# The first batch's first transform folded on VectorE and TensorE, with another order behind it

## The chip, the cores and the metric

The kernel runs on one core of one Trainium2 chip. The metric is the device time of one execution in microseconds (us); lower is better. A core has five engines that run their own instruction queues: TensorE (PE in the rows, with PEld its weight loads), VectorE (DVE), ScalarE (ACT), GpSimd (POOL) and SP (SyncE), which here only issues DMAs. Every engine takes its instructions in program order, and a semaphore wait of one instruction holds back those behind it.

## The reference

Eight batches of 3072 positions with 256 channels pass through three layers; all is fp32.

```python
X = np.fft.rfft(x, axis=1)                       # x: (8, 3072, 256)
y = np.fft.irfft(X * (filt_r + 1j * filt_i)[None], n=3072, axis=1)
...
h = np.maximum(x @ w_in, 0.0)                    # (24576, 256) @ (256, 2048)
x = h * h @ w_out                                # (24576, 2048) @ (2048, 256)
...
logits = x @ phi                                 # 32 slots, 8 experts of 4
d = softmax(logits, axis=0)                      # over all tokens
slot_input = (d.T @ x).reshape(8, 4, 256)
slot_out[e] = np.maximum(slot_input[e] @ w1[e], 0) @ w2[e]
out = softmax(logits, axis=1) @ slot_out
```

The second and third layers see the whole (24576, 256) array.

## The kernel before, in words

The kernel has a start-up of about 60 us, a main loop over 384 pairs of w_in column blocks (`pair`, with `layer`, `square`, `turn_h`, `logit`), and an end with the experts. The transforms of batches 1 to 7 are spread over the main loop as streams of events; batch 0 has to be transformed in the start-up, because the main loop's first chunk needs it. Only batch 0, with the constants it uses, is touched here.

The 3072-point transform is done as 128 x 24: index n1 has 128 values (on partitions), n2 has 24. Batch 0 passes these stages, each an event with a time key:

- `load_u` loads x by n2 into tiles `x` (line 160); `mm_at` multiplies each 128 x 128 block of x, as the stationary operand, with the 128 x 128 matrix `ca` (line 275): this is the first transform, and its result comes out with the channels on partitions. `evac_at` copies it into `AT` (lines 284 and 286).
- `mm_t` turns blocks of `AT` back (line 294), `evac_t` copies (line 299); group i of eight holds 16 of the 128 first frequencies.
- `mm_b` is the 24-point transform (line 309), `filt` four VectorE products with the filter for each group i (line 320), `join` the sums on GpSimd (line 329), `mm_g` the inverse 24-point transform (line 349), `evac_g` four ScalarE copies (line 362). Group 7 has no join: its `mm_g` has twice the matmuls.
- `store_g` stores the groups' rows to DRAM tensors `Gu` (groups 0 to 5) and `Gz` (6 and 7) (line 371), and `load_gi` loads the tile `gi` back in another order (line 378). Then `mm_ai` (line 501), `lead_ai` (ScalarE, line 510) and `rest_ai` (VectorE, line 522) make the main loop's first operand `xo`, and `layer` begins (lines 615 to 622); `square` is the relu (line 627). A `warm` of matmuls without use (lines 402 and 494) runs at the beginning and while gi is awaited.

Beside these, the start-up converts the weights, which arrive as 64-bit floats. For each tile of w_in and w_out `conv` runs one ScalarE copy (line 987, k = 0) and then five VectorE operations (lines 944, 945, 948, 949, 1002, k = 1 to 5); `split_wi` then makes a high part on ScalarE (line 1014) and a low part on VectorE (line 1012). `WI` and `WO` hold their time keys; the first two tiles of w_in are converted in halves.

The order on each engine is written by hand. `put0(t, fn, ...)` files an event under the key t, and at the end all events are called in the order of their keys; a key is not a time that anything waits for, it only says what stands ahead of what in program order. Of the keys of `fft_events`, F(i) = 20 + 2.45 i.

PSUM has eight banks; `bank0(k)` names one, and a matmul group waits until the last reader of its bank is done. `mm_at(u)` takes bank u % 8, `mm_t` banks 4 to 7, `mm_b(i)` two of banks 0 to 3, `mm_g(i)` four banks by a table.

The batches behind the first are folded already (`fold_x`, `mm_a`): a row n1 and the row n1 + 64 are added for the even frequencies and subtracted for the odd ones, which leaves two products over 64 rows.

Of the kernel before, what the change touches and what calls it, by code (L numbers as in the profile page):

```python
# [6 lines left out]
F32 = mybir.dt.float32  # L7
# [31 lines left out]
def body(tc, x, cA, cAf, fwp, fwd, ivp, inv, flt, cst, w_in, w_out, phi, w1, w2, out):  # L39
# [23 lines left out]
    def F(i):  # L63
# [4 lines left out]
        ([.35, 27.6], [[16.6, 17.1, 17.11, 17.12, 17.13, 17.14], [34.2, 40.4, 40.41, 40.42, 40.43, 40.44]], 47.2, 47.58),  # L68
        ([30.1], [[41, 46, 46.1, 46.2, 46.3, 46.4]], 47.3, W + .1),
        ([W + 2.2], [[W + 4] + [W + t for t in (5.9, 6.4, 7.3, 7.8, 8.5)]], W + 9.1, W + 10.1),  # L70
# [62 lines left out]
    def fft_events(b, pl, put, TA, TB, TG, n, st):  # L133
# [22 lines left out]

        def load_u(u, m=2):
            sl, n = divmod(2 * u, 4)
            st["x", sl] = st["big"][sl // 4][:, sl % 4]
            sync.dma_start(out=st["x", sl][:, n:n + m], in_=xv[:, 2 * u:2 * u + m, :])  # L160

# [108 lines left out]
        def mm_at(u):  # L270
            st["at", u] = p = bank0(u % 8)
            for k in range(2):
                for m in range(2):
                    o = 128 * (2 * k + m)
                    pe.matmul(
                        p[:, o:o + 128], st["x", u // 2][:, 2 * (u % 2) + m, 128 * k:128 * k + 128], st["ca"],
                        start=True, stop=True,
                    )

        def evac_at(u):  # L280
            o = st["AT"][:, :, :, 2 * u:2 * u + 2]
            p = st.pop(("at", u)).rearrange("p (k n q) -> p k q n", k=2, n=2)
            if u == 2:
                vec.tensor_copy(o, p)
            else:
                act.activation(out=o, in_=p, func=ACTF.Copy)

# [46 lines left out]
        def mm_g(i):  # L334
            v = st.pop(("iv", i))
            st["g", i] = p = [bank0(k) for k in ((4, 5, 6, 7), (0, 1, 4, 5), (2, 3, 6, 7))[(i > 3) + (i > 5)]]
            if i < 7:
# [66 lines left out]
        if b == 0:  # L404

            st["wz"] = cv.tile([128, 512], F32, tag="wx", name="wz", bufs=1)
            st["ca"] = pl().tile([128, 128], F32, name="ca")
            put(0.01, load_ca)
            put(0.05, warm, st["wz"][:, 0:128], 7)
            st["AT"] = one("AT", [128, 2, N1, 32])  # L410
            st["big"] = [G["big"].tile([128, 4, 4, D], F32, tag=f"h{n}", name="x", bufs=1) for n in "AB"]
            put(0.04, lambda: vec.memset(st["AT"][:, :, :, N2:], 0.0))
            for u in range(6):
                put(.2 + .01 * u, load_u, u)
            for u in range(6, 12, 2):
                put((.27, .28, .31)[u // 2 - 3], load_u, u, 4)
            put(.32, load_k, C_ID, C_SS)
            put(.46, load_k, C_I, C_ID)
            put(.461, load_k, C_SS, C_END)
            for u in range(12):  # L420
                put(4.2 + .98 * u, mm_at, u)
                put(5.4 + .98 * u, evac_at, u)
            put(.37, load_c, 0)
            put(.45, load_c, 1)
            put(.43, load_i, 0)
            put(.455, load_i, 1)
            put(29.3, negate)
            for i in range(8):
                put((.38, .4, .42, .44)[i] if i < 4 else F(i - 4) + 2.6, load_f, i)
                T = (16.8, 17.2, 20, 22.4, 24.9, 25.3, 27.4, 27.8)[i]  # L430
                for s in range(2):
                    put(T + .1 * s, mm_t, i, s)
                    put(T + .3 + .1 * s, evac_t, i, s)
                put(F(i) - 1.2, mm_b, i)
                for r in range(2):
                    put(F(i) + 1.25 * r, filt, i, r)
                    if i < 7:
                        put(F(i) + 1.3 + 1.25 * r, join, i, r)
                put((29.85, 32.3, 34.75, 37.2, 39.9, 41.5, 44.6, 40.5)[i], mm_g, i)
                T = (31.1, 33.6, 36.1, 38.6, 41.2, 44.7, 45.9, 42.4)[i]  # L440
                for c in range(4):
                    put(T, evac_g, i, c)
                put(T + 1.25, store_g, i)
            put(45.0, load_gi, sync, 0, "Gu", 0, 64)
            return
# [31 lines left out]
    def out_events(b, st, late):  # L477

        def load_g(g):
            if b + g:  # L480
                t = G["mlp"].tile([128, 4, D], F32, tag="gin", name="gin", bufs=2)
                src, o = (st["G1"], 0) if (b, g) == (0, 1) else (st["G"], 4 * g - 8 * (b == 0))
                sync.dma_start(out=t, in_=src[:, o:o + 4, :])
                st["gi", g] = t
                return
            st["load_gi"](sync, 0, "Gu", 64, 96)
            st["load_gi"](sync, 96, "Gz", 16, 32)
            st["load_gi"](sync, 96, "Gz", 0, 16)

# [977 lines left out]
def _constants():  # L1467
# [11 lines left out]
    cA = np.tile(a[:64].reshape(64, 2, 64), (2, 1, 1))  # L1479
    cAf = a.reshape(N1, 8, 2, 4, 2).transpose(0, 1, 3, 2, 4).reshape(N1, N1)  # L1480
    ci = np.where(ri[None, :] == 0, np.cos(ph), -np.sin(ph)).T.copy()
# [134 lines left out]
```

## Time and profile before

| | |
|---|---|
| median of 3 runs | 1836.63 us (1831.43 to 1837.27) |
| profiled execution | 1833.53 us |
| its span, first to last instruction | 1831.6 us |
| mean granted TensorE clock | 0.997 of full speed |
| TensorE busy | 1799.2 us, 98% of the span |
| VectorE, ScalarE, GpSimd busy | 66%, 57%, 43% |

All times in rows are microseconds from the span's start. A timeline row merges neighbouring instructions of one line; its second number is from the first one's start to the last one's end. fp32 matmuls appear as two instructions each, apart from transposes. The granted clock is in parts of 2.4 GHz.

### The profile page before, as it was taken

Reading aid. Unit: us, or ns where it says so; the run is one execution under the profiler, and the core shown is the slowest. Engines: PE = TensorE matmul, PEld = TensorE weight load, DVE = VectorE, ACT = ScalarE, POOL = GpSimd, SP = SyncE. Lnnn points to the kernel's source line nnn. Section 1 sums busy time; section 2 is a strip of 40 time slices with the busy share of each in tenths; the row PEclk is TensorE's granted clock in tenths of the full one; section 3 lists DMA queues with packets and bytes.
Section 4 is the critical chain, followed back from the end, with each engine's and each line's share of the span. In section 5 each row is a group of like instructions: output and inputs, shape, how many; then the busy total and the mean of one; then the engine's idle time right before and its main releaser. Section 6 shows DMA issues by size and latency. Waiting matters only on the chain.

```text
span 1831.6 us, 41877 instructions
## 1 busy us (share of the span) xinstructions
PE 1799.2 (98%) x16338; PEld 1195.2 (65%) x16338; DVE 1200.7 (66%) x2252; ACT 1046.5 (57%) x1942; POOL 782.1 (43%) x818
## 2 busy tenths in 40 slices
PE   9899999999999999999999999999999999999986
PEld 7666666666676666666666666666666676666555
DVE  7856766776576656667567666666566756556567
ACT  6755555555654664655555566465555565555556
POOL 4144543544354534445345543445344433333234
PEclk9999999999999999999999999999999999999999
DMA  8669989888888888888878888788888766675889
GB/s 315 207 182 285 254 231 266 255 220 226 250 211 227 222 250 214 220 233 232 235 210 231 222 234 243 207 224 237 236 214 226 189 177 179 171 201 155 302 305 384
DMA packets 236419, 425.00 MB, mean 232 GB/s; under 512 B 25536, under 2 KB 94784, under 8 KB 233408
## 3 DMA queue, kind: packets, MB, share of 16 engines
q1 hardware_dynamic: 235352, 421.13, 80.8%
q8 instruction: 130, 2.13, 0.5%
q10 hardware_dynamic: 728, 1.15, 0.2%
q14 instruction: 65, 0.53, 0.1%
q0 software_dynamic: 144, 0.07, 0.0%
HBM read 151.71 MB, written 77.59 MB: 125 GB/s over the span
## 4 chain that ended last, share of the span: by engine, by line
PE 93%; DVE 2%; DMA 2%; ACT 1%; issue 1%; SPq 1%; POOL 0%; ACTq 0%; DVEq 0%
PE p L620 20%; PE p L622 19%; PE p L621 19%; PE L L689 10%; PE S L820 5%; PE sd L820 3%; PE sd L309 3%; PE sd L228 3%; PE sd L175 2%; PE sd L537 1%; PE y L537 1%; DVE ct L1245 1%; PE pt L1234 1%; PE pt L1447 1%; PE sd L349 1%
## 5 line engine op out<-in xcount | busy, mean ns | idle before, releaser
L648 DVE STREAM_TRANSPOSE hT<-h 128x512 f32<-128x512 f32 x736 | 490.4, 694 | 320.3 <-ACT h L629 302.0
L631 POOL TENSOR_TENSOR h<-h 128x512 f32<-128x512 f32 x375 | 391.5, 1044 | 591.9 <-ACT h L627 559.1
L627 ACT ACTIVATE h<-p 128x512 f32<-128x512 f32 x768 | 458.8, 597 | 323.2 <-PE p L622 305.1
L620 PE MATMUL p<-xo,wiH 128*128 128x512 f32 x1534 | 619.6, 404 | 0.8 <-ACT h L627 0.6
L622 PE MATMUL p<-xo,wiL 128*128 128x512 f32 x1534 | 605.9, 395 | 0.0
L621 PE MATMUL p<-xo,wiH 128*128 128x512 f32 x1534 | 605.2, 395 | 0.1
L620 PEld LDWEIGHTS p<-xo,wiH 128*128 128x128 f32 x1534 | 288.3, 188 | 126.3 <-issue 35.8
L622 PEld LDWEIGHTS p<-xo,wiL 128*128 128x128 f32 x1534 | 288.5, 188 | 68.3
L621 PEld LDWEIGHTS p<-xo,wiH 128*128 128x128 f32 x1534 | 288.8, 188 | 61.9 <-DVE xo L522 0.5
L629 ACT ACTIVATE h<-h 128x512 f32<-128x512 f32 x393 | 248.4, 632 | 12.5
L329 POOL TENSOR_TENSOR u<-u 128x256 f32<-128x256 f32 x224 | 160.9, 740 | 131.0 <-DVE u L320 117.2
L689 PE MATMUL L<-h,wf 128*32 128x512 f32 x1536 | 187.9, 599 | 0.5 <-ACT h L629 0.4
L320 DVE TENSOR_TENSOR u<-sd,f 128x512 f32<-128x512 f32 x240 | 151.8, 670 | 39.1 <-PE sd L309 39.0
L571 POOL TENSOR_TENSOR xo<-gin,xo 128x512 fp32r<-128x512 f32 x90 | 116.9, 1310 | 101.6 <-ACT xo L564 101.6
L556 DVE TENSOR_TENSOR gin<-gin,sd 128x512 f32<-128x512 f32 x90 | 61.8, 687 | 92.6 <-ACT gin L547 91.1
L547 ACT ACTIVATE gin<-y 128x512 f32<-128x512 f32 x28 | 16.7, 597 | 161.0 <-PE sd L537 161.0
L689 PEld LDWEIGHTS L<-h,wf 128*32 128x32 f32 x1536 | 40.1, 109 | 94.9 <-issue 92.1
L820 PE MATMUL S<-hd,eT 128*32 128x512 f32 x896 | 101.3, 592 | 0.0
L166 POOL TENSOR_TENSOR f<-f 128x512 f32<-128x512 f32 x42 | 54.2, 1291 | 85.6 <-DVE u L165 79.0
L564 ACT ACTIVATE xo<-gin 128x512 fp32r<-128x512 f32 x90 | 53.3, 621 | 41.3 <-DVE gin L556 41.3
L796 DVE STREAM_TRANSPOSE eT<-et 32x128 f32<-32x128 f32 x184 | 72.3, 393 | 1.9
L820 PEld LDWEIGHTS S<-hd,eT 128*32 128x32 f32 x896 | 29.1, 110 | 67.0 <-issue 67.0
(168 smaller groups left out, 1732.2 us busy)
## 6 DMA issues: line engine op xcount, KB each, us to landing
hd<-hT SPq DMA_DIRECT2D x736, 256.0 KB
f<-flt SPq DMA_DIRECT2D x28, 1024.0 KB
gin<-G SPq DMA_DIRECT2D x47, 512.0 KB
out<-w1t SPq DMA_DIRECT2D x22, 1024.0 KB
f<-x SPq DMA_DIRECT2D x84, 256.0 KB
S<-f SPq DMA_DIRECT2D x42, 512.0 KB
f<-S SPq DMA_DIRECT2D x112, 192.0 KB
G<-f SPq DMA_DIRECT2D x112, 192.0 KB
```

The costliest lines, as they stand in the source:

```text
L320: vec.tensor_tensor(out=u, in0=p.rearrange("p (h d) -> p h d", d=D), in1=f[:, 2 * r + k:2 * r + k + 1, :].to_broadcast([128, 2, D]), op=AL ...
L329: gps.tensor_tensor(out=a[:, h, :], in0=a[:, h, :], in1=b[:, 1 - h, :], op=ALU.add if h else ALU.subtract)
L571: gps.tensor_tensor(out=lo, in0=st["gi", g][:, k::2, :], in1=hi, op=ALU.subtract)
L620: pe.matmul(p, wh, x[:, 0, kk, :], start=(kk == 0), stop=False)
L621: pe.matmul(p, wh, x[:, 1, kk, :], start=False, stop=False)
L622: pe.matmul(p, wl, x[:, 0, kk, :], start=False, stop=(kk == 1))
L627: act.activation(out=h, in_=p, func=ACTF.Relu, scale=2.0 ** -8)
L629: act.activation(out=h, in_=h, func=ACTF.Square)
L631: gps.tensor_tensor(out=h, in0=h, in1=h, op=ALU.mult)
L648: vec.transpose(hT[c, f // 8][:, f // 4 % 2, :, o:o + 128], h2[P, k].rearrange("p (b t) -> p b t", b=4))
L689: pe.matmul(lg[c][32 * n:32 * n + 32, :], wf[:, f, :], h2.pop((P + n // 2, n % 2)), start=(f < 4), stop=(f >= FT - 4), tile_position=(0, 3 ...
L820: pe.matmul(S[32 * n:32 * n + 32, :], e[:, 32 * t:32 * t + 32], v, start=(t == 0), stop=(t == 3), tile_position=(0, 32 * n),)
```

## The change

For batch 0 the first transform is folded as well. x is loaded in six units u, each with rows n1 under 64 and over 64 side by side, and with four n2, two on the upper and two on the lower 64 partitions (12 loads of 256 KB instead of six of 256 KB and three of 512 KB). For u = 0 to 3 VectorE adds and subtracts the two halves (`fold_u`), and TensorE multiplies the results by 64 x 64 tiles. For u = 4 and 5 TensorE does the sum itself: it accumulates both halves, with a third block of `ca` that holds the negated odd columns. Each unit fills two PSUM banks, and ScalarE evacuates both (`evac_at(u, g)`; before, unit 2 of twelve was copied by VectorE).

The keys of `mm_t`, `evac_t`, `mm_b`, `mm_g` and `evac_g` are earlier; the groups' last three come as 5, 7, 6 instead of 7, 5, 6, and groups 5 to 7 use other banks. The ScalarE copy of the third tile of w_in has key 43 instead of 41. gi is loaded in two pieces: 96 rows of `Gu` ahead of group 6's store in the queue, and 32 rows of `Gz`; before, it was 64 and 32 rows of `Gu` and twice 16 of `Gz`.

```diff
--- before.py
+++ after.py
@@ -66,7 +66,7 @@
     WI = [
         ([.26, .3], [[8.4, 9.9, 9.91, 9.92, 9.93, 9.94], [13.26, 13.3, 13.31, 13.32, 13.33, 13.34]], 20.4, 40.3),
         ([.35, 27.6], [[16.6, 17.1, 17.11, 17.12, 17.13, 17.14], [34.2, 40.4, 40.41, 40.42, 40.43, 40.44]], 47.2, 47.58),
-        ([30.1], [[41, 46, 46.1, 46.2, 46.3, 46.4]], 47.3, W + .1),
+        ([30.1], [[43, 46, 46.1, 46.2, 46.3, 46.4]], 47.3, W + .1),
         ([W + 2.2], [[W + 4] + [W + t for t in (5.9, 6.4, 7.3, 7.8, 8.5)]], W + 9.1, W + 10.1),
     ]
     WO = [
@@ -154,10 +154,19 @@
                         out=t[64 * g:64 * g + 64, k].rearrange("p (h n) d -> p h n d", h=2), in_=xh[:, :, n:n + 2, :]
                     )
 
-        def load_u(u, m=2):
-            sl, n = divmod(2 * u, 4)
-            st["x", sl] = st["big"][sl // 4][:, sl % 4]
-            sync.dma_start(out=st["x", sl][:, n:n + m], in_=xv[:, 2 * u:2 * u + m, :])
+        def load_u(u):
+            st["x", u] = t = st["big"][u // 4][:, u % 4]
+            for g in range(2):
+                n = 4 * u + 2 * g
+                sync.dma_start(
+                    out=t[64 * g:64 * g + 64].rearrange("p (h n) d -> p h n d", h=2), in_=xh[:, :, n:n + 2, :]
+                )
+
+        def fold_u(u):
+            t = st["x", u]
+            st["eo", u] = [small(k) for k in ((("u0", "u1"), ("u2", "u3"), ("u4", "u5"), ("u6", "u7"))[u])]
+            for o, op in zip(st["eo", u], (ALU.add, ALU.subtract)):
+                vec.tensor_tensor(out=o, in0=t[:, 0:2], in1=t[:, 2:4], op=op)
 
         def fold_x(s, k):
             t = st["x", s][:, k]
@@ -268,22 +277,32 @@
                 sync.dma_start(out=f[:, r:r + 2], in_=flt[i, :, r:r + 2])
 
         def mm_at(u):
-            st["at", u] = p = bank0(u % 8)
+            st["at", u] = p = [bank0((2 * u + g) % 8) for g in range(2)]
+            ca, t = st["ca"], st["x", u]
+            if ("eo", u) in st:
+                terms = [[(a, 0, 64 * e)] for e, a in enumerate(st.pop(("eo", u)))]
+            else:
+                terms = [[(t, 0, 64 * e), (t, 2, 128 * e)] for e in range(2)]
             for k in range(2):
-                for m in range(2):
-                    o = 128 * (2 * k + m)
-                    pe.matmul(
-                        p[:, o:o + 128], st["x", u // 2][:, 2 * (u % 2) + m, 128 * k:128 * k + 128], st["ca"],
-                        start=True, stop=True,
-                    )
-
-        def evac_at(u):
-            o = st["AT"][:, :, :, 2 * u:2 * u + 2]
-            p = st.pop(("at", u)).rearrange("p (k n q) -> p k q n", k=2, n=2)
-            if u == 2:
-                vec.tensor_copy(o, p)
-            else:
-                act.activation(out=o, in_=p, func=ACTF.Copy)
+                for n in range(2):
+                    for e, term in enumerate(terms):
+                        for m, (a, h, c) in enumerate(term):
+                            for g in range(2):
+                                rows = slice(64 * g, 64 * g + 64)
+                                for d in range(2):
+                                    o, q = 128 * (2 * k + n) + 64 * e, 128 * k + 64 * d
+                                    pe.matmul(
+                                        p[g][64 * d:64 * d + 64, o:o + 64], a[rows, h + n, q:q + 64],
+                                        ca[rows, c:c + 64],
+                                        start=(m == 0), stop=(m == len(term) - 1), skip_group_check=True,
+                                        tile_position=(64 * g, 64 * d),
+                                    )
+
+        def evac_at(u, g):
+            n = 4 * u + 2 * g
+            o = st["AT"][:, :, :, n:n + 2]
+            p = st["at", u][g].rearrange("p (k n q) -> p k q n", k=2, n=2)
+            act.activation(out=o, in_=p, func=ACTF.Copy)
 
         def mm_t(i, s):
             st["tp", i, s] = p = bank0(4 + (2 * i + s) % 4)
@@ -333,7 +352,7 @@
 
         def mm_g(i):
             v = st.pop(("iv", i))
-            st["g", i] = p = [bank0(k) for k in ((4, 5, 6, 7), (0, 1, 4, 5), (2, 3, 6, 7))[(i > 3) + (i > 5)]]
+            st["g", i] = p = [bank0(k) for k in ((4, 5, 6, 7), (0, 1, 4, 5), (6, 7, 0, 1), (6, 7, 0, 1), (2, 3, 4, 5))[max(0, i - 3)]]
             if i < 7:
                 y = [st.pop(("y", i, r)) for r in range(2)]
                 terms = [[(v[:, r, k, :], y[r][:, k, :]) for r in range(2)] for k in range(2)]
@@ -404,22 +423,24 @@
         if b == 0:
 
             st["wz"] = cv.tile([128, 512], F32, tag="wx", name="wz", bufs=1)
-            st["ca"] = pl().tile([128, 128], F32, name="ca")
+            st["ca"] = pl().tile([128, 192], F32, name="ca")
             put(0.01, load_ca)
             put(0.05, warm, st["wz"][:, 0:128], 7)
             st["AT"] = one("AT", [128, 2, N1, 32])
             st["big"] = [G["big"].tile([128, 4, 4, D], F32, tag=f"h{n}", name="x", bufs=1) for n in "AB"]
             put(0.04, lambda: vec.memset(st["AT"][:, :, :, N2:], 0.0))
             for u in range(6):
-                put(.2 + .01 * u, load_u, u)
-            for u in range(6, 12, 2):
-                put((.27, .28, .31)[u // 2 - 3], load_u, u, 4)
+                put((.2, .21, .22, .27, .28, .31)[u], load_u, u)
             put(.32, load_k, C_ID, C_SS)
             put(.46, load_k, C_I, C_ID)
             put(.461, load_k, C_SS, C_END)
-            for u in range(12):
-                put(4.2 + .98 * u, mm_at, u)
-                put(5.4 + .98 * u, evac_at, u)
+            for u in range(6):
+                T = 4.2 + 1.6 * u
+                if u < 4:
+                    put(T - .2, fold_u, u)
+                put(T, mm_at, u)
+                for g in range(2):
+                    put(T + 1.2 + .1 * g, evac_at, u, g)
             put(.37, load_c, 0)
             put(.45, load_c, 1)
             put(.43, load_i, 0)
@@ -427,21 +448,21 @@
             put(29.3, negate)
             for i in range(8):
                 put((.38, .4, .42, .44)[i] if i < 4 else F(i - 4) + 2.6, load_f, i)
-                T = (16.8, 17.2, 20, 22.4, 24.9, 25.3, 27.4, 27.8)[i]
+                T = (15, 15.4, 19.8, 22, 24, 24.4, 26.9, 28.9)[i]
                 for s in range(2):
                     put(T + .1 * s, mm_t, i, s)
                     put(T + .3 + .1 * s, evac_t, i, s)
-                put(F(i) - 1.2, mm_b, i)
+                put((17, 20.8, 22.9, 25.9, 27.9, 30.6, 33, 35.2)[i], mm_b, i)
                 for r in range(2):
                     put(F(i) + 1.25 * r, filt, i, r)
                     if i < 7:
                         put(F(i) + 1.3 + 1.25 * r, join, i, r)
-                put((29.85, 32.3, 34.75, 37.2, 39.9, 41.5, 44.6, 40.5)[i], mm_g, i)
-                T = (31.1, 33.6, 36.1, 38.6, 41.2, 44.7, 45.9, 42.4)[i]
+                put((29.9, 32, 34.2, 36, 37.2, 38.3, 40.9, 39.3)[i], mm_g, i)
+                T = (31, 33.1, 35.3, 37.1, 38.3, 39.4, 42.4, 41.4)[i]
                 for c in range(4):
                     put(T, evac_g, i, c)
                 put(T + 1.25, store_g, i)
-            put(45.0, load_gi, sync, 0, "Gu", 0, 64)
+            put(43.2, load_gi, sync, 0, "Gu", 0, 96)
             return
 
         for s, (TL, TF, T) in enumerate(TA):
@@ -483,9 +504,7 @@
                 sync.dma_start(out=t, in_=src[:, o:o + 4, :])
                 st["gi", g] = t
                 return
-            st["load_gi"](sync, 0, "Gu", 64, 96)
-            st["load_gi"](sync, 96, "Gz", 16, 32)
-            st["load_gi"](sync, 96, "Gz", 0, 16)
+            st["load_gi"](sync, 96, "Gz", 0, 32)
 
         def warm():
 
@@ -1477,7 +1496,8 @@
     a[:, 0] = 1.0
     a[:, 1] = alt
     cA = np.tile(a[:64].reshape(64, 2, 64), (2, 1, 1))
-    cAf = a.reshape(N1, 8, 2, 4, 2).transpose(0, 1, 3, 2, 4).reshape(N1, N1)
+    cAf = a[:64].reshape(64, 8, 2, 4, 2).transpose(0, 1, 3, 2, 4).reshape(64, N1)
+    cAf = np.tile(np.concatenate([cAf, -cAf[:, 64:]], axis=1), (2, 1))
     ci = np.where(ri[None, :] == 0, np.cos(ph), -np.sin(ph)).T.copy()
     ci[0] = 1.0
     ci[1] = alt
```

## Rows read from the trace of the kernel before

**Rows 1.** Windows of ten us: length, busy us of each engine (instructions), granted clock, DMA share.

```profile
70.00:80.00 10.00, 10.00 (x64) 6.99 (x63) 9.82 (x14) 8.14 (x14) 2.54 (x2) 1.00 0.79 255
```

**Rows 2.** Chain that ended last, 47 to 62 us: start us, us, what.

```profile
47.81 2.47 DMA Gu<-x
...
51.66 3.98 DMA gi<-Gz
...
58.31 0.43 PE p L615
...
61.11 0.23 PE p L621
```

**Rows 3.** Timeline of VectorE: start, us, line, shapes, count, [idle before <- releaser].

```profile
18.43 0.43 DVE L944 TENSOR_SCALAR wa<-wa 128x512 uint32<-128x512 uint32 x1
...
20.81 0.69 DVE L1002 TENSOR_TENSOR wa<-wa,we 128x512 f32<-128x512 f32 x1
21.42 0.68 DVE L320 TENSOR_TENSOR u<-sd,f 128x512 f32<-128x512 f32 x1
...
38.99 0.69 DVE L320 TENSOR_TENSOR u<-sd,f 128x512 f32<-128x512 f32 x1 [0.66 <-PE sd L309]
...
46.10 0.69 DVE L944 TENSOR_SCALAR wa<-wa 128x1024 uint32<-128x1024 uint32 x1
...
53.06 1.22 DVE L945 SCALAR_TENSOR_TENSOR wa<-wt,wa 128x1024 uint32<-128x1024 uint32 x1
57.62 0.69 DVE L522 TENSOR_TENSOR xo<-sd,xo 128x512 fp32r<-128x512 f32 x1 [3.33 <-ACT xo L510]
```

**Rows 4.** Timeline of ScalarE, start-up.

```profile
10.52 1.10 ACT L286 ACTIVATE AT<-sd 128x512 f32<-128x512 f32 x2
...
17.72 0.68 ACT L987 ACTIVATE wa<-wt 128x512 f32<-128x512 f32 x1
18.57 2.07 ACT L299 ACTIVATE x<-sd 128x512 f32<-128x512 f32 x4 [0.17 <-PE sd L294]
...
41.69 1.20 ACT L987 ACTIVATE wa<-wt 128x1024 f32<-128x1024 f32 x1
...
44.70 3.63 ACT L362 ACTIVATE x<-sd 128x256 f32<-128x256 f32 x12 [0.71 <-PE sd L349]
...
51.33 1.06 ACT L1014 ACTIVATE wiH<-wa 128x1024 fp32r<-128x1024 f32 x1 [0.22 <-DVE wa L1002]
```

**Rows 5.** Timeline of TensorE, start-up.

```profile
4.33 6.36 PE L275 MATMUL sd<-ca,x 128*128 128x128 f32 x48
11.19 6.00 PE L275 MATMUL sd<-ca,x 128*128 128x128 f32 x48 [0.49 <-DMA x<-x]
17.88 1.97 PE L294 MATMUL sd<-cst_t,AT 128*128 128x128 f32 x16 [0.70 <-ACT AT L286]
...
30.91 1.12 PE L349 MATMUL sd<-u,iv 32*64 32x256 f32 x32
...
55.77 2.53 PE L501 MATMUL sd<-cst_t,gi 128*128 128x128 f32 x16 [2.94 <-DMA gi<-Gz]
```

**Rows 6.** Timeline of TensorE around one mm_y of the main loop.

```profile
416.62 0.27 PE L537 MATMUL y<-cst_t,gin 64*64 64x64 f32 x2
...
417.71 1.98 PE L228 MATMUL sd<-u,iv 32*64 32x256 f32 x64
```

**Rows 7.** Timeline of SP's queue, 43.5 to 44 us.

```profile
43.93 0.26 SPq L371 DMA_DIRECT2D Gu<-x  x1
```

**Rows 8.** Timeline of GpSimd, start-up.

```profile
22.78 19.34 POOL L329 TENSOR_TENSOR u<-u,v 128x256 f32<-128x256 f32 x28 [22.33 <-DVE v L320]
```

**Rows 9.** Windows of one us, columns as in rows 1.

```profile
48.00:49.00 1.00, 0.62 (x2) 0.47 (x3) 0.93 (x3) 0.33 (x3) 0.00 (x0) 1.00 0.83 247
...
57.00:58.00 1.00, 1.00 (x9) 1.00 (x7) 0.38 (x1) 0.59 (x1) 0.00 (x0) 0.56 0.05 16
...
59.00:60.00 1.00, 1.00 (x3) 0.82 (x3) 1.00 (x2) 0.00 (x0) 0.00 (x0) 0.50 0.00 0
```

## Prediction

> **What bounds the kernel now.** I read four views in this order. First the ten-microsecond windows: from 70 to 80 us TensorE is busy throughout [rows 1], and over the span 98%. Only the start-up, the first 60 us, is touched by this change, so what moves the first relu of the main loop moves the end by as much. Second the chain of waits through the end of the start-up: the store of the last result groups (2.47 us), the fetch of gi (landing 55.64 us), mm_ai, then the first layer's matmuls from 58.31 us [rows 2]. Read alone, this says that the fetch bounds. Third, VectorE by time: it works without a hole from the first filt at 21.42 us until L945 ends at 54.28 us, but for a hole of 0.66 us ahead of the eighth filt (0.73 against the pace of the filts, 0.60), then idles 3.33 us and takes rest_ai at 57.62 us [rows 3]. So an earlier gi is worth 3.33 us at most (4.06 with the hole closed), and only if VectorE itself is not later. What starts VectorE's long run is therefore what matters, and for that I read ScalarE [rows 4] and TensorE [rows 5].
>
> **First transform, removed and added.** Before: 48 fp32 products, 96 instructions, 6.36 + 6.00 us with a 0.49 us wait for x, ending 17.19 us; the one evacuation left brings mm_t to 17.88 us [rows 5]. After: four folded units of 32 products (64 instructions) and two unfolded ones of 64 products (128 instructions). The same form stands in mm_y: 64 instructions of 64x64 start between 416.62 us and the next line's start at 417.71 us, the pipeline's turn-over included [rows 6]; I take 1.0 us for 64, so 1.0 us a folded unit and 2.0 us an unfolded one. The sum is 8 us for 12.4: TensorE saves 4.
>
> But a folded unit waits for both VectorE sums. L1002 has the same form, 0.69 us and about 0.72 from start to start [rows 3], so a fold takes 1.44 us. The order and bytes of the loads are as before, in quarter-megabyte pieces; the fourth unit is the data on which TensorE waited until 11.19 us [rows 5]. Six old units had landed and were multiplied by 10.69 us [rows 5], so the first three folds fit in ahead. Fourth fold: 11.2 + 1.44 = 12.65 us. Its matmuls can run their first eighth on the sum alone, so they end at 12.65 + 0.87 = 13.5; the two unfolded units at 15.5 and 17.5 us (the last data had landed by 15.2, since the old TensorE run from 11.19 us never stopped). Then two evacuations, where the old order had one left: 0.55 each in a row of two [rows 4], with start-up 1.15: mm_t starts at 18.7 us against 17.88. The four microseconds saved on TensorE end in the wait for x and the folds, and the first transform is 0.8 us later. More x loads (three more issues on SP) and a weight tile half as large again hide in the time until 11.19 us, where TensorE waits for x anyway; without that cover, the issues would cost some 0.3 us each, as one on SP's queue does [rows 7].
>
> **The moved order, and what it costs.** VectorE runs in program order: three converted half-tiles of w_in, then the filts. The third conversion starts from a ScalarE copy, L987. Before, the copy stood ahead of evac_t and ran at 17.72 us; the five VectorE operations followed from 18.43 to 21.50 us and the first filt at 21.42 us [rows 3, 4]. After, mm_t and evac_t have earlier order keys (15 to 15.8) and the copy keeps 16.6: it now stands behind four evacuations of mm_t. From mm_t's start at 17.88 us to the end of the fourth at 20.64 us were 2.76 us [rows 4, 5]; the copy adds 0.63 with its start. So the copy ends at 18.7 + 2.76 + 0.63 = 22.1 us, the five operations take 3.07 us, and the first filt starts at 25.15 us: 3.7 us late. (VectorE's own work would allow it at 12.65 + 3 x 3.07 = 21.9 us, plus the wait of the second conversion, whose copy now stands behind the fifth unit's evacuations: 23.5.) GpSimd's joins follow the filts: 28 in 19.34 us from 22.78 us before [rows 8], so they end at 45.9 us.
>
> **The tail.** Filts and conversions: 54.28 - 0.73 + 3.7. I count the 0.73 us hole as gone, since mm_b(7) is now placed earlier and waits only for the sixth filt's banks. The eighth filt ends at 44.4 us. A mm_g of 32 instructions takes 1.0 to 1.1 us [rows 5], so mm_g(7), twice as long, takes 2.1 behind it, and mm_g(6) 1.0 beside evac_g(7); ScalarE then has eight evacuations, 0.3 us each by the twelve in 3.63 us [rows 4]: evac_g(6) ends at 44.4 + 2.1 + 2.4 = 48.9 us. Before it ended at 48.33. The new order of groups and banks thus wins back 3.1 of the 3.7 us there. The ScalarE copy of the third w_in tile, 1.20 us [rows 4], moved from ahead of evac_g(4) to behind evac_g(6), ends at 50.0 us; VectorE is ready for it at 46.10 - 0.73 + 3.7 = 49.1 [rows 3] and waits 0.9. So that conversion starts 3.9 us later than before, and rest_ai cannot start ahead of 54.28 + 3.9 = 58.2 us.
>
> The fetch: stores issued at 48.9, landed 2.47 later, one issue of 0.4, and a landing of between 2.47 (as the store) and 3.98 (as the old last piece, with two w_out loads issued by ScalarE in front of it) [rows 2, 4]: gi at 54.2 to 55.8 us, against 55.64. I take 54.2, as those w_out loads now come behind split_wi at 51.33 + 3.9 [rows 4]. One half of mm_ai follows (1.0 to 1.3 us): 57.1 at the latest. ScalarE is free at 51.33 + 1.06 + 3.9 = 56.3. Both lie ahead of 58.2, so the two-piece fetch is hidden behind VectorE. SP's stores could be late too: the eighth of fourteen went out at 43.93 us before [rows 7]. Should that shift by the whole 3.7, seven more issues of 0.3, two store landings one behind the other and a fetch bring gi to about 57.2 and its first half to 58.2: still a tie.
>
> **Sum.** rest_ai 58.2 against 57.62: +0.6. The warm-up matmuls begin when the last evacuation frees its bank and end some 4.5 us later, at 53.4, so TensorE is idle for about a microsecond, not 2.94 [rows 5], and the last two matmuls ahead of the first relu run at 0.23 instead of 0.43 us each [rows 2, 9]: -0.4. Total +0.2 us. The profiled execution took 1833.53 us, its span 1831.6 with 1.9 us around it; the median of the runs shown lies 3.1 above it. Against the median: 1836.63 + 0.2 = 1836.8 us. Bounds of this case: the 0.9 us wait absent and mm_t at 18.2, -1.2; clock gain absent and mm_t half a microsecond late, +1.3.
>
> **Rivals.**
> *Faster: the transform is ready early.* For: TensorE's work shrinks by 4 us. It decides from mm_t at 17.1 us or less; then the third copy no longer holds VectorE up, the first filt starts at about 23.6 us, and the sum is 0.2 - 1.5 = -1.3, or -2.2 if the 0.9 goes with it: 1834.4 to 1835.4 us. Against: the fourth fold and 4.9 us of matmuls behind it. A gain over 0.3% (5.5 us) needs rest_ai at 52.1, ahead of VectorE's own work. Chance 0.12.
>
> *Slower: TensorE's clock.* The folds leave TensorE idle between units, longest from about 10.7 to 12.65 us. Before, it idled for 2.94 us until 55.77 us [rows 5], and the granted clock then read 0.56 and, two microseconds on, 0.50, the low one of its two levels, 1.2 GHz [rows 9]. With the microsecond between alike, that lost 0.44 + 0.5 + 0.5 = 1.4 us of work. If it falls on the unfolded units, mm_t starts at 20.1 us and the sum is 0.2 + 1.4 = +1.6; twice, +3.0. Against: at 48 us, where TensorE was busy for 0.62 of the microsecond, the clock stayed at 1.00. Chance 0.2: 1838.2 us. [...]
>
> *Slower: the small tiles don't overlap.* If only two of the four tiles work at once, 64 instructions take 1.9 us and 128 take 3.75; mm_t starts at 12.65 + 1.75 + 7.5 + 1.15 = 23.05 us, +4.35: 1841.2 us. Against: mm_y is the same form and order [rows 6]. Chance 0.06. [...]
>
> **Numbers.** Likeliest, 0.62: no change, 1836.8 us (its own range 1834.5 to 1839). The runs before lie between 1831.43 and 1837.27, so about 0.3%, 5.5 us, is what this kernel's measurement can tell from none. The 8-in-10 range takes in the faster case less the runs' scatter and the clock case twice: 1831.8 to 1841.0. Faster by over 0.3%: 0.04. Slower: 0.08, from the tile case and a double clock loss with a late fetch. Within: 0.88.
>
> **What would show it.** Right: L275's successor ends near 17.5 us and the first mm_t near 18.7; L987's third copy behind four evac_t; the first filt at 25 us; the hole ahead of the eighth filt gone; gi landed ahead of VectorE's last conversion, and rest_ai waiting for VectorE's own work, near 58 us. Wrong: a first filt ahead of 23 us (then faster by that much), granted clock of 0.5 between 12 and 20 us, a unit of 64 instructions over 1.2 us, or rest_ai waiting again for mm_ai.

## The result, and the profile after

The changed kernel takes 1857.22 us (median of 4 runs, 1855.12 to 1859.6), the kernel before 1835.16 us beside it (4 runs): a ratio of 1.0123, 95% interval 1.010 to 1.0146. It is 22 us slower where no change (1836.8 us, at most 1841.0) was forecast. The profiled execution took 1859.6 us with a span of 1857.7.

TensorE by time comes first, in the columns of [rows 5]. "issue" in the brackets means that the engine waited for nothing that the profile shows.

```profile
6.61 7.17 PE L294 MATMUL sd<-ca,u 64*64 64x64 f32 x192 [2.19 <-DVE u L169]
15.21 0.34 PE L294 MATMUL sd<-ca,u 64*64 64x64 f32 x8 [1.43 <-DVE u L169]
15.81 0.38 PE L294 MATMUL sd<-ca,u 64*64 64x64 f32 x9 [0.26 <-DVE u L169]
17.57 1.45 PE L294 MATMUL sd<-ca,u 64*64 64x64 f32 x44 [1.37 <-issue]
...
18.90 2.13 PE L294 MATMUL sd<-ca,x 64*64 64x64 f32 x79
24.66 3.35 PE L294 MATMUL sd<-ca,x 64*64 64x64 f32 x127 [3.63 <-issue]
30.67 1.50 PE L294 MATMUL sd<-ca,x 64*64 64x64 f32 x49 [2.66 <-issue]
33.26 3.68 PE L313 MATMUL sd<-cst_t,AT 128*128 128x128 f32 x16 [1.09 <-ACT AT L305]
...
77.04 2.02 PE L520 MATMUL sd<-cst_t,gi 128*128 128x128 f32 x16 [1.92 <-DMA gi<-Gz]
```

The first mm_t (L313 now) starts at 33.26 us instead of 17.88 [rows 5]: 15.4 of the 22 us are lost in the first transform. Three times TensorE stops for 1.37 to 3.63 us without a wait that the profile shows. The first stop comes after 192 + 8 + 9 matmul instructions, the next two 127 further on each (the first 127 are 44, four in two short rows that are left out here, and 79).

VectorE, beside [rows 3]:

```profile
5.87 1.29 DVE L169 TENSOR_TENSOR u<-x 128x512 f32<-128x512 f32 x2 [2.72 <-DMA x<-x]
...
14.47 1.29 DVE L169 TENSOR_TENSOR u<-x 128x512 f32<-128x512 f32 x2 [2.51 <-DMA x<-x]
...
38.18 0.43 DVE L963 TENSOR_SCALAR wa<-wa 128x512 uint32<-128x512 uint32 x1 [7.17 <-ACT wa L1006]
...
41.17 0.68 DVE L339 TENSOR_TENSOR u<-sd,f 128x512 f32<-128x512 f32 x1
...
49.51 0.69 DVE L339 TENSOR_TENSOR u<-sd,f 128x512 f32<-128x512 f32 x1 [1.08 <-PE sd L328]
...
55.65 0.69 DVE L339 TENSOR_TENSOR u<-sd,f 128x512 f32<-128x512 f32 x1 [1.26 <-PE sd L328]
...
60.60 0.69 DVE L339 TENSOR_TENSOR u<-sd,f 128x512 f32<-128x512 f32 x1
...
71.64 0.69 DVE L963 TENSOR_SCALAR wa<-wa 128x1024 uint32<-128x1024 uint32 x1 [4.45 <-ACT wa L1006]
...
79.75 0.68 DVE L541 TENSOR_TENSOR xo<-sd,xo 128x512 fp32r<-128x512 f32 x1
```

The fourth fold waits for x until 14.47 us. The first filt is 19.75 us late (41.17 against 21.42), the first rest_ai 22.13 (79.75 against 57.62). So 15.4 us arise ahead of mm_t, 4.4 between mm_t and the first filt, 2.4 behind it.

ScalarE has a part in the last two: both times the copy for which VectorE waits stands behind evacuations (four of L318 end at 37.58, eight of L381 begin at 68.29), as the changed keys have it. The relu L646 is 21.31 us later than L627 before (60.92).

```profile
37.47 0.68 ACT L1006 ACTIVATE wa<-wt 128x512 f32<-128x512 f32 x1
...
68.29 2.32 ACT L381 ACTIVATE x<-sd 128x256 f32<-128x256 f32 x8 [0.49 <-PE sd L368]
70.42 1.19 ACT L1006 ACTIVATE wa<-wt 128x1024 f32<-128x1024 f32 x1
...
82.23 0.60 ACT L646 ACTIVATE h<-p 128x512 f32<-128x512 f32 x1 [2.53 <-PE p L637]
```

Windows, columns as in [rows 1], first of ten us and then of two:

```profile
10.00:20.00 10.00, 6.71 (x222) 5.87 (x221) 5.43 (x9) 3.76 (x8) 0.00 (x0) 0.86 1.06 255
...
18.00:20.00 2.00, 2.00 (x88) 2.00 (x84) 0.71 (x2) 0.85 (x2) 0.00 (x0) 0.50 1.12 221
...
22.00:24.00 2.00, 0.00 (x0) 0.00 (x0) 0.00 (x0) 0.00 (x0) 0.00 (x0) 1.00 1.04 379
24.00:26.00 2.00, 1.34 (x50) 1.34 (x53) 0.00 (x0) 0.00 (x0) 0.00 (x0) 0.51 1.05 384
...
34.00:36.00 2.00, 2.00 (x11) 2.00 (x10) 0.00 (x0) 1.20 (x2) 0.00 (x0) 0.50 0.02 6
```

The same ten microseconds of the kernel before:

```profile
10.00:20.00 10.00, 8.68 (x79) 7.92 (x85) 7.36 (x13) 7.80 (x14) 0.00 (x0) 1.00 1.04 399
```

The DMA engines are as busy as before (1.06 and 1.04), but move 255 GB/s instead of 399. Behind each stop TensorE's clock is granted at 0.50, and it is still there in mm_t, where TensorE is busy for all of 2 us (34 to 36 us). Read in tenths of a us up to 76 us, it is 1.00 or 0.50 in both kernels, but for the ten tenths in which it changes (0.58 to 0.95).

This leaves three suspects for the 15.4 us: the loads onto halves of the partitions, the supply of instructions behind the stops (512 matmul instructions for 96), and the clock.

### The profile page after: what moved, and what is told of

It reads as the page before. It is cut to its first block, busy times and chain, and to the rows that moved or that the text cites. A ratio compares the mean times of both kernels' runs of the same rounds, so it can differ in the third digit from the quotient of the medians.

```text
span 1857.7 us, 42737 instructions
## 1 busy us (share of the span) xinstructions
PE 1808.5 (97%) x16754; PEld 1200.4 (65%) x16754; DVE 1205.4 (65%) x2259; ACT 1047.7 (56%) x1943; POOL 783.2 (42%) x818
## 4 chain that ended last, share of the span: by engine, by line
PE 90%; DVE 3%; DMA 2%; issue 2%; ACT 1%; SPq 1%; ACTq 0%; DVEq 0%
PE p L639 20%; PE p L641 18%; PE p L640 18%; PE L L708 9%; PE S L839 5%; PE sd L839 3%; PE sd L328 3%; PE sd L237 3%; PE sd L184 2%; PE y L556 1%; PE sd L556 1%; DVE ct L1264 1%; PE pt L1253 1%; PE pt L1466 1%; PE sd L769 1%
## 5 line engine op out<-in xcount | busy, mean ns | idle before, releaser
L646 ACT ACTIVATE h<-p 128x512 f32<-128x512 f32 x768 | 459.2, 598 | 330.0 <-PE p L641 311.6
L566 ACT ACTIVATE gin<-y 128x512 f32<-128x512 f32 x28 | 16.7, 597 | 161.0 <-PE sd L556 161.0
```

The lines of the kernel that those rows point to most:

```text
L646: act.activation(out=h, in_=p, func=ACTF.Relu, scale=2.0 ** -8)
```

## The experiments

The total of a single execution says little here: 23 runs of the kernel before beside e9 to e12 lie between 1831.03 and 1838.64 us, 17 beside e15 between 1830.44 and 1839.76. The verdicts rest on stage times in the trace; only e11, e12 and e15 have enough executions (11 or 12) to compare totals. Stage times scatter too: e5, e11, e12 and e15 share one first transform, and their mm_t starts between 17.66 and 19.00 us, so a shift of about 1 us says little. Line numbers shift by a few between these kernels.

**e1, the loads alone.** The kernel before, each x load split in an upper and a lower half of the partitions:

```diff
-            sync.dma_start(out=st["x", sl][:, n:n + m], in_=xv[:, 2 * u:2 * u + m, :])
+            for g in range(2):
+                rows = slice(64 * g, 64 * g + 64)
+                sync.dma_start(out=st["x", sl][rows, n:n + m], in_=xv[rows, 2 * u:2 * u + m, :])
```

> The kernel before, with each load of x split into two of 64 partitions and nothing else changed. If loads of half the partitions are what delays x (the changed kernel's fourth unit landed at 14.4 us instead of 11.2): the wait of TensorE for x, 0.49 us until 11.19 us before, ends at 14 us or later, mm_t starts at 21 us or later instead of 17.88, and DMA moves under 260 GB/s while x loads. If the rival is right, that the delay comes from TensorE's instruction fetch and other traffic and not from the form of the loads: x lands within 0.7 us of before, mm_t starts by 18.6 us. The total moves by less than the shift of mm_t, since VectorE's 3.3 us of idle time ahead of rest_ai takes it up: 0 to +4 us in the first case, within 1 us in the second.

TensorE by time:

```profile
16.80 5.71 PE L277 MATMUL sd<-ca,x 128*128 128x128 f32 x32 [4.88 <-DMA x<-x]
24.27 2.02 PE L277 MATMUL sd<-ca,x 128*128 128x128 f32 x16 [1.76 <-DMA x<-x]
26.98 1.97 PE L296 MATMUL sd<-cst_t,AT 128*128 128x128 f32 x16 [0.69 <-ACT AT L288]
```

mm_t came 9.1 us later than before with the same products, the first relu 9.14 (70.06); 1846.44 us in all. The rate from 10 to 20 us was 243 GB/s. The expectation that VectorE's idle time would take most of it up missed: the shift came through whole.

**e5 and e6, width against size.** The kernel before with x in twelve loads of 256 KB, which is the change's count, size and order: over all partitions (e5) or over half of them (e6).

```diff
+            for g in range(2):
+                n = 4 * u + 2 * g
+                sync.dma_start(out=t[:, 2 * g:2 * g + 2], in_=xv[:, n:n + 2, :])   # e5
+                rows = slice(64 * g, 64 * g + 64)
+                sync.dma_start(out=t[rows], in_=xv[rows, 4 * u:4 * u + 4, :])      # e6 in its place
```

> The kernel before with x in twelve loads of 256 KB over all 128 partitions (pieces of 2 KB), in the order of the changed kernel; nothing else changed. A control for the next run: as many loads, of the same size, so the same waits for a free place among the loads in flight. If the half of the partitions is the cause of the late x, this run is like before: TensorE's wait for x ends at 11 to 12.3 us, mm_t at 17.5 to 19 us, total within 2 us of before. If the number and size of the loads are the cause: mm_t at 21 us or later.

> As the run above, but each of the twelve 256 KB loads covers 64 partitions (pieces of 4 KB). If half the partitions is the cause: DMA moves 190 to 260 GB/s while x loads although the engines are busy, TensorE's last wait for x ends after 20 us, mm_t at 22 to 28 us, total +5 to +14 us. If number and size are the cause: the same as the run above.

The ten-microsecond window of e5, and behind it that of e6:

```profile
10.00:20.00 10.00, 8.33 (x83) 7.56 (x89) 7.45 (x14) 7.99 (x15) 0.00 (x0) 1.00 1.05 393
```

```profile
10.00:20.00 10.00, 7.65 (x62) 7.14 (x61) 4.78 (x9) 5.39 (x10) 0.00 (x0) 1.00 1.04 256
```

e5 had mm_t at 17.77 us, e6 at 24.50: half the partitions cost 6.7 us, and neither the number nor the size of the loads does.

**e7, halves on two queues.** The changed kernel, every second half issued by ScalarE (`(sync, act)[g].dma_start(`), so that upper and lower halves travel side by side.

> The changed kernel, with the lower halves of x (partitions 0 to 63) loaded from SP's queue and the upper halves from ScalarE's, so that both are in flight side by side. If a load of half the partitions is slow because it reaches only a part of the ways into SBUF: DMA over 300 GB/s while x loads, the fourth unit lands by 12.5 us instead of 14.4, the first filt 3 to 8 us earlier than 41.17 us, total -3 to -8 us against the changed kernel. If the pieces or the distance between them in HBM are the cause: x lands when it did, total within 2 us.

The fourth unit came at 14.38 us, mm_t at 33.00 instead of 33.26, and the rate from 10 to 20 us was 278 GB/s: refuted as a cure.

**e13, every other partition.** As e6, but with `rows = slice(g, 128, 2)`.

> As e6 (x in twelve 256 KB loads of 64 partitions by 4 KB), but each load takes every other partition instead of an upper or lower half. If it matters which partitions a load fills, and the upper or lower 64 alone are slow, the rate from 10 to 20 us goes back from 256 to some 390 GB/s and the first mm_t comes at about 18 us, as in e5. If 64 partitions are slow whichever they are, or the 4 KB rows are, the rate stays near 260 GB/s and mm_t at about 24.5 us.

```profile
10.00:20.00 10.00, 7.26 (x61) 6.75 (x60) 5.49 (x10) 6.18 (x11) 0.00 (x0) 1.00 1.02 391
```

The rate is back at 391 GB/s and mm_t at 19.74 us. So 64 partitions are not slow as such; 64 that lie in one half are (256 GB/s in e6). The 2 us left against e5 (0.7 to 2.1 against the four kernels with e5's loads) were not followed further.

**e3, more instructions alone.** The kernel before, each 128 x 128 product cut in four of 128 x 32: 192 products for 48, nothing else.

```diff
+                    for c in range(4):
+                        q = 128 * k + 32 * c
+                        pe.matmul(
+                            p[32 * c:32 * c + 32, o:o + 128], st["x", u // 2][:, 2 * (u % 2) + m, q:q + 32], st["ca"],
+                            start=True, stop=True, skip_group_check=True, tile_position=(0, 32 * c),
+                        )
```

> The kernel before, each 128x128 product of mm_at cut into four of 128x32 tiles: 192 products instead of 48, the same columns and the same loads. If TensorE's instructions come in blocks of about 256 (128 loads and 128 matmuls) that are fetched late while the DMA engines are full: stops of 1 to 4 us without a releaser inside L275 after each 127 or 128 matmuls, two or three of them, mm_t at 21 to 27 us. If only the loads' form matters: no stop, mm_t within 1 us of 17.88. Total: up to +6 us in the first case, within 1 in the second.

```profile
12.96 3.84 PE L277 MATMUL sd<-ca,x 128*32 128x128 f32 x127 [0.67 <-issue]
19.22 1.52 PE L277 MATMUL sd<-ca,x 128*32 128x128 f32 x48 [2.42 <-issue]
21.46 1.97 PE L296 MATMUL sd<-cst_t,AT 128*128 128x128 f32 x16 [0.72 <-ACT AT L288]
```

The stops appear with full-width loads too, again 127 matmul instructions apart; mm_t is 3.6 us late, the first relu 2.86.

**e4, half the instructions.** The changed kernel with 64 x 128 tiles: 128 products instead of 256, each of two matmul instructions.

```diff
-                                for d in range(2):
-                                    o, q = 128 * (2 * k + n) + 64 * e, 128 * k + 64 * d
...
+                                o, q = 128 * (2 * k + n) + 64 * e, 128 * k
+                                pe.matmul(
+                                    p[g][:, o:o + 64], a[rows, h + n, q:q + 128], ca[rows, c:c + 64],
+                                    start=(m == 0), stop=(m == len(term) - 1), skip_group_check=True,
+                                    tile_position=(64 * g, 0),
+                                )
```

> The changed kernel with tiles of 64x128 instead of 64x64 in mm_at: 128 products instead of 256, everything else the same. If instruction fetch is the main cost: the stops inside L294 shrink from three (1.37, 3.63 and 2.66 us) to one or two, the first filt comes 5 to 9 us earlier than 41.17 us, total -5 to -9 us against the changed kernel. If the loads are the main cost: the last matmul of L294 moves by less than 2 us, since x lands when it did.

TensorE by time, and its ten-microsecond window:

```profile
19.79 13.87 PE L293 MATMUL sd<-ca,x 64*128 64x64 f32 x128
34.82 3.67 PE L311 MATMUL sd<-cst_t,AT 128*128 128x128 f32 x16 [1.16 <-ACT AT L303]
```

```profile
20.00:30.00 10.00, 10.00 (x97) 10.00 (x98) 1.41 (x3) 2.74 (x5) 0.00 (x0) 0.50 1.04 386
```

A miss: the stops are gone, but TensorE runs at the low clock from 10 to 36 us, 108 ns a matmul instruction (13.87 / 128), and mm_t comes at 34.82 us, 1.6 us later than in the changed kernel. As the pace changed with the count, e4 doesn't price the stops.

**e9, fewer instructions, folded.** The changed kernel with all six units folded on VectorE (`fold_u` for u = 4 and 5 too): 384 matmul instructions, not 512.

> The changed kernel, with all six units of the first transform folded on VectorE: 384 instructions of matrix work instead of 512. If TensorE's supply of instructions and its low clock in the unfolded units set when the transform is ready, the stops of TensorE for no shown reason fall from three to two, the last product ends 4 to 7 us earlier than 32.1 us, and the first filt comes as much earlier. If the slow loads alone set it, the last unit still lands at about 22.5 us and the transform can't be ready before 24.5 us; a gain under 1.5 us speaks for that, or for the price of two more folds on VectorE.

VectorE's last fold, and TensorE:

```profile
22.83 1.29 DVE L169 TENSOR_TENSOR v<-x 128x512 f32<-128x512 f32 x2 [2.95 <-DMA x<-x]
```

```profile
23.67 2.58 PE L294 MATMUL sd<-ca,v 64*64 64x64 f32 x64 [1.96 <-DVE v L169]
27.44 3.41 PE L313 MATMUL sd<-cst_t,AT 128*128 128x128 f32 x16 [1.19 <-ACT AT L305]
```

One stop is left (1.44 us, until 17.58), mm_t gains 5.8 us, the first relu 7.0 (75.26), and the total is 1848.2 us. Now the last unit of x, at 22.83 us, sets the transform.

**e8, the copy's place.** The changed kernel with the third ScalarE copy ahead of mm_t's evacuations again (key 14.9 instead of 16.6).

> The changed kernel, with the ScalarE copy of the third half-tile of w_in ahead of mm_t's evacuations again (key 14.9 instead of 16.6). By the prediction's step the first filt then waits only for mm_b(0): 38.3 to 38.7 us instead of 41.17. As TensorE is late there too, less of it may reach the end: total -1 to -3 us against the changed kernel. If the place of the copy costs nothing: the first filt within 0.5 us of 41.17.

```profile
38.81 0.69 DVE L339 TENSOR_TENSOR u<-sd,f 128x512 f32<-128x512 f32 x1 [2.05 <-PE sd L328]
```

mm_t stood where it was (33.16 us), the first filt came at 38.81 instead of 41.17 and waits for mm_b now, the first relu came 3.4 us earlier.

**e2 and e10, the second half of the change.** e2 is the kernel before with the diff's keys and banks behind the transform, the two-piece gi and key 43 for the third w_in tile's copy; the first two groups keep their mm_t keys of before. e10 gives that copy back its key 41.

```diff
-        ([30.1], [[43, 46, 46.1, 46.2, 46.3, 46.4]], 47.3, W + .1),
+        ([30.1], [[41, 46, 46.1, 46.2, 46.3, 46.4]], 47.3, W + .1),
```

> The kernel before with the second half of the change alone: keys of mm_b, mm_g, evac_g and of mm_t from the third group on, banks, order 5, 7, 6, fetch in two pieces, third copy's key 43; the first transform and the loads are the old ones. By the prediction's working VectorE bounds here: rest_ai at 53.5 to 55 us instead of 57.62, gi landed by 54, total -2 to -4 us. By the rival, that the new order itself is part of the loss: rest_ai at 58 us or later, total +0 to +4 us.

> The kernel before with the second half of the change, as in e2, but the third w_in tile's copy put ahead of the copies of the last products (key 41 instead of 43). If ScalarE's order makes VectorE's wait there (3.77 us in e2), the wait falls to 1.2 us or less, the first rest_ai comes at about 57 us instead of 59.59, and the first relu 1.5 to 2.5 us earlier than in e2. If gi sets the end of the stage, the first relu moves by less than 0.7 us.

VectorE of e2, then TensorE of e10:

```profile
51.48 0.69 DVE L942 TENSOR_SCALAR wa<-wa 128x1024 uint32<-128x1024 uint32 x1 [3.77 <-ACT wa L985]
...
59.59 0.68 DVE L520 TENSOR_TENSOR xo<-sd,xo 128x512 fp32r<-128x512 f32 x1
```

```profile
57.51 2.82 PE L499 MATMUL sd<-cst_t,gi 128*128 128x128 f32 x16 [2.96 <-DMA gi<-Gz]
```

e2's first relu was 1.15 us late, and 0.57 of that stood already in its mm_t (18.45 us), which the edit doesn't touch: the second half wins nothing. In e10 the wait shrank to 0.93 us, as expected, but then gi was late: rest_ai at 59.36, the first relu at 62.67 instead of 62.07. The rival was right.

**e14, the last piece of gi.** The kernel before with its last two loads of 16 rows as one of 32.

```diff
-            st["load_gi"](sync, 96, "Gz", 16, 32)
-            st["load_gi"](sync, 96, "Gz", 0, 16)
+            st["load_gi"](sync, 96, "Gz", 0, 32)
```

> The kernel before, with the last 32 rows of gi fetched in one piece instead of two of 16, and nothing else. If the single piece is what made gi late in e10 and e12, mm_ai starts 1 us or more later than 55.77 us. If gi was late there because of the order of the stores and the bigger first piece ahead of them, mm_ai stays within 0.5 us of 55.77.

mm_ai came at 53.54 us, earlier than either case had it, and the first relu at 57.86; the whole last piece is not what made gi late.

**e11, e12 and e15, timed.** e11 is e5's kernel, e15 adds e14's edit, and e12 gives e5's kernel the change's banks, its order 5, 7, 6 and its two pieces, with key 41 and keys of its own for the last groups.

> The kernel before with x in twelve loads of 256 KB over all 128 partitions, in the change's order of units, and nothing else. Its first relu came 3.4 us earlier than before in one look. If that head start survives to the end: 1 to 3 us faster, a ratio of 0.998 to 0.9995. If later waits take it back: the same within 1 us.

> The kernel before with x in twelve full-width loads, gi fetched in two pieces, the change's banks behind the transform, and keys of my own: the third w_in tile's copy at 41, ahead of the last copies. If what the change does behind the transform is sound once its order on ScalarE is mended: the first rest_ai at about 54 us and a total 2 to 4 us under the kernel before. Rival: VectorE sets the end of that stage anyway, and the time is that of e11.

> The two edits of the kernel before that each brought the first relu some 3 us forward, together: x in twelve full-width loads (e11) and the last 32 rows of gi in one piece (e14). VectorE's own work allows the first rest_ai at about 54 us, so the first relu can't come ahead of 56 us, 4 to 5 us earlier than before. If such a head start reaches the end, the time is 3 to 5 us under the kernel before (ratio 0.997 to 0.9985). If it is taken back in the main loop, as in e11, the interval takes in 1.

VectorE of e12:

```profile
59.95 0.69 DVE L519 TENSOR_TENSOR xo<-sd,xo 128x512 fp32r<-128x512 f32 x1 [5.88 <-ACT xo L507]
```

| | first relu, us | median, us | ratio (95%) |
|---|---|---|---|
| e11 | 57.85 | 1834.47 | 1.0003 (0.9993 to 1.0013) |
| e12 | 63.2 | 1837.68 | 1.0017 (1.0008 to 1.0027) |
| e15 | 58.77 | 1834.17 | 0.9997 (0.9986 to 1.0009) |

No version beats the kernel before. e12 loses 3 us to a late gi. e11 and e15 start the main loop 2 to 3 us earlier and end together with it: both expectations of a gain missed, and where a lead that small goes stays open.

## Why the prediction was wrong

**The step that failed** is the first transform: "The order and bytes of the loads are as before ... the fourth unit is the data on which TensorE waited until 11.19 us", and with it mm_t at 18.7 us. Bytes and order were as before; the partitions that each load fills were not. And the matmuls behind that unit, 4.9 us in the sum, had no term for the supply of instructions. In the chain that ended last of the changed kernel, the pieces from the fourth unit's fold to the last product are these (start us, us, what):

```profile
14.47 0.13 DVE u L169
...
15.81 0.38 PE sd L294 x9
16.20 1.37 issue
17.57 3.46 PE sd L294 x127
21.03 3.63 issue
24.66 3.35 PE sd L294 x127
28.00 2.66 issue
30.67 1.43 PE sd L294 x47
```

mm_t came 14.6 us behind its forecast. The fourth unit and its fold make 3.1 of them (done at 15.76 us, not at 12.65), the three stops 7.7, and the matmuls between the stops 3.7 (8.6 us for 4.9, 312 matmul instructions).

The late x is worth more than its 3.1 us once the stops are gone: in e9, with one stop and no unfolded units, mm_t is still 9.6 us later than before, as the last unit lands near 22.8 us, against 15.2 in the prediction. e9 gives back only 5.8 us, for two stops and the two unfolded units. e1 and e6 show that the halves alone make x late (mm_t by 9.1 and 6.7 us), and e13 that it is the half, not the count. The two causes lie side by side, so their prices do not add up, and no run had the 512 matmul instructions with loads at the full rate.

What the runs show of the loads is their rate from 10 to 20 us: onto one half 243 GB/s in e1, 255 in the changed kernel and 256 in e6, each with loads of w_in among them; onto every other partition 391 (e13), onto all 393 (e5). Two half loads under way at once did not make up for it (e7, 278 GB/s). Why a half is slow no run shows; the prediction weighed the bytes and the order alone.

**The stops were no rival.** The prediction priced a matmul and not the supply of matmuls. On the page the queue named instruction has packets of 16 KB; their number and MB for the kernel before, and behind it for the changed one:

```profile
q8 instruction: 130, 2.13, 0.5%
q8 instruction: 133, 2.18, 0.5%
```

Weight loads counted, e4 has 320 instructions of TensorE more than the kernel before, e3 and e9 576, the changed kernel 832, and the pages count 131, 132, 132 and 133 packets: about one for 256 instructions. The stops stand 254 instructions apart, and each ends 2.3 to 2.9 us behind such a packet (the changed kernel, e3, e7, e8, e9). In the changed kernel's DMA view, cut in tenths of a us, the packets stand at 14.8, 22.1 and 28.0 us, and the stops end at 17.57, 24.66 and 30.67; in e3 they stand at 10.6 and 16.7, and the stops end at 12.96 and 19.22. By these times TensorE waits there for the next packet of its instructions.

What counts is the pace, not the number of instructions alone: e4 passes its 209th matmul instruction too, at about 28.6 us (an estimate from its row), but 127 of them take it 13.7 us, and the packet stands at 17.1. In e9 the second such packet stands at 22.2 us, while TensorE waits for x until 23.67. That the full DMA engines make the packets late is argued: no run had such a burst beside idle ones. With a DMA share near 1.0, the longest of these stops took 3.63 us.

**The clock** was a rival at 0.2 for 1.4 to 3.0 us, with the idle time that the folds leave as its reason. In the changed kernel it fell behind the wait for the fourth unit, with the first stop: 1.00 from 14 to 16 us, 0.81 from 16 to 18, 0.50 from 18 to 20. In e7 and e8, with the same matmuls, it read 0.50 from 10 to 20 us, ahead of the first stop, and mm_t came no later for that (33.00 and 33.16 us). Of the 3.7 us above some 2.2 are the low clock, by an estimate: the 312 instructions would take 6.4 us at the 20 ns below. Behind the transform mm_t's two runs took 3.68 us where they took 1.97 [rows 5]. No run took the low clock away alone; in e4, where it read 0.50 from 10 to 36 us, nothing was left of the saving in instructions.

**The small tiles** overlapped, though less well than in [rows 6]: from 10 to 11 us 49 matmul instructions ran in 1.00 us at full clock, some 20 ns each (one lasts 312 ns in the mean up to 16 us), so 1.3 us a folded unit and not 1.0, or 1.5 us over the 312. A unit over 1.2 us and a clock of 0.50 between 12 and 20 us were both among the prediction's own signs of being wrong.

**The copies.** That the copy "now stands behind four evacuations of mm_t" was right: 2.9 us between mm_t and the first filt were predicted on top of its delay, 4.4 came, 2.4 of them the copy (e8), the rest the slow matmuls of mm_t and mm_b.

**The tail** has three wrong terms. The hole ahead of the eighth filt did go (60.60 us, without a wait), but two others came, 1.08 us ahead of the fourth and 1.26 ahead of the sixth; in e2 there are 0.82 us ahead of the sixth and 1.31 ahead of the eighth. And the copy with key 43 made VectorE wait 4.45 us (3.77 in e2), not 0.9. "The new order of groups and banks thus wins back 3.1 of the 3.7 us there" did not hold: before, the last evacuation ended 26.9 us behind the first filt, in the changed kernel 29.4, in e2 28.5.

**gi hidden behind VectorE** was right, for the reason given: the w_out loads now come behind it, and mm_ai began 2.43 us after gi's last issue (74.61 to 77.04). But it was hidden only because VectorE was late; once that was mended (e10, e12), gi was what rest_ai waited for. With the w_out loads issued ahead of the last piece, mm_ai began 3.84 and 4.50 us after that piece's issue (e10, e12), much as before, where the piece took 3.98 [rows 2]; with them behind it, 2.54 (e2), 2.43 (the changed kernel) and at most 2.37 (e14, where another piece landed last). e2 and the changed kernel have the 384 KB piece and the new order of groups as well, so neither is what makes the landing late. From the last store on SP to gi's last issue it was much the same in all: 3.3 us before, 3.2 in e14, 3.5 in e10, 3.9 in e12 and in the changed kernel.

**The first premise**, that what moves the first relu moves the end by as much, held for a large shift (21.3 us there, 22.1 in the medians) and not for the leads of 2 to 3 us in e11 and e15. The profiled executions drift apart by another 4.8 us behind the first relu (26.1 at the end), the medians by 0.8: that difference is within the scatter of the runs.

## What to carry to other kernels

A change of layout that keeps bytes and order of a load can still take a third off its rate (255 GB/s for 399 here): before costing a transform in tiles of 64 rows, see which partitions each load fills, and compare GB/s at equal DMA share. Count instructions as well as their time: with a DMA share near 1.0 a burst of short matmuls waited here up to 3.63 us for its own program, as the packets of the instruction queue show. And mend an order on one engine only after asking which wait ends next, since here a fetch stood 3 us behind the copy that hid it.

## What had not been expected of the hardware

With DMA share near 1.0, loads onto the upper or lower 64 partitions ran at 243 to 256 GB/s (e1, the changed kernel, e6), onto every other one or all of them at 391 to 399 (e13, e5, the kernel before). TensorE stopped for 0.67 to 3.63 us every 127 matmul instructions where these took some 20 to 30 ns each, and each stop ended 2.3 to 2.9 us behind a packet of the instruction queue. And in e4 it stayed at a granted clock of 0.50 from 10 to 36 us, although it was busy for 24.8 of the 26 us.
